# Reordering the head of batch 0 so that norms run ahead of the exps, with 1/rms in PSUM and MLP chunks begun in the score banks

## The chip, the cores and the metric

The kernel runs on one core of one Trainium2 chip. The time is the device time of one execution in microseconds (us), the median of several runs. Each experiment was timed in turns with the kernel before, on the same chip, and is quoted as a ratio to it.

Engines: PE (matmul), PEld (PE's weight loads), DVE (vector), ACT (scalar), POOL (GpSimd), SP (issues DMAs). Each works through its own instructions in order. A *stop* or a *hole* is a stretch in which PE runs nothing.

## The reference, cut to what matters

```python
def _attn_ref(q, k, v, g_q, g_k):          # 8 batches, 12 heads, 448 rows, 64 columns
    def rmsnorm(x, g):
        rms = np.sqrt(np.mean(x * x, axis=-1, keepdims=True) + 1e-06)
        return x / rms * g
    q_n, k_n = (rmsnorm(q, g_q), rmsnorm(k, g_k))
    scores = np.matmul(q_n, k_n.transpose(0, 1, 3, 2)) / np.sqrt(64)
    ...                                    # softmax over the last axis: attn
    return np.matmul(attn, v)

def _moe_ref(x, U, V, w_ch1, w_ch2):       # x: 8 x 448 x 768, w_ch1: 768 x 3072, w_ch2: 3072 x 768
    xt = x.transpose(0, 2, 1)
    h = xt @ U @ V
    u = x + h.transpose(0, 2, 1)
    ch = np.maximum(u @ w_ch1, 0.0) @ w_ch2
    return u + ch
```

Inputs and output are float32.

## The kernel before: the parts that matter here

Two heads make a *pair*, six pairs a batch, two pairs a *tile* of q, k and v loads. A pair needs squares, a sum over the head's columns (`reduce`), 1/rms by Ln and Exp (`rsqrt`), the scaling of q and k (`scale`), a transpose, the scores, the exps, and the product with v (`values`). Batch b+1's attention is woven between the MLP matmuls of batch b. Only batch 0 has nothing to hide behind: pairs 0 to 5 run alone first. That stretch is the *head*. *Mixing* is the U, V part of `_moe_ref`, which makes u; w1 and w2 are `w_ch1` and `w_ch2`. An MLP *chunk* is the six w1 matmuls for 128 of the 3072 hidden columns, with a relu behind them. A *bank* is a PSUM buffer for matmul results; the score banks are those of `ps_s`.

```python
ps_mm = ctx.enter_context(tc.tile_pool(name="ps_mm", bufs=3, space=bass.MemoryType.PSUM))
ps_s  = ctx.enter_context(tc.tile_pool(name="ps_s",  bufs=2, space=bass.MemoryType.PSUM))   # 2 x 2 banks
ps_o  = ctx.enter_context(tc.tile_pool(name="ps_o",  bufs=1, space=bass.MemoryType.PSUM))
...
def scale(p):                               # both inputs in SBUF
    ...
    nc.vector.tensor_tensor(qkns[p]..., qk_of[t][0:SP, a]..., rstds[t][:, a]....to_broadcast([SP, 4, NJ, D]), OP.mult)

def dma_transposes(p):                      # pairs 6 and up
    nc.sync.dma_start_transpose(out=qkTs[p % NQ]..., in_=qkns.pop(p)...)

def gains(p):                               # after a DMA transpose
    qT = blocks(p)[:, :, 0]
    nc.vector.tensor_scalar(qT, qT, gg, None, OP.mult)
...
def pair(p):                                # the head, pairs 0 to 5
    scores(p, (1,)); expo(p, 0)
    if p: values(p - 1, 0)
    if p < 4: scale(p + 1)
    ...
    scores(p, (2,)); expo(p, 1)
    if p < 5: transposes(p + 1)             # on PE
    if p: values(p - 1, 1, ps_mm)
    ...
    if p == 2:                              # the same in pairs 0 and 4
        for a in range(2): reduce(2, a)     # two pairs of norms at once
        rsqrt(2, slice(0, 2))
        ...
    scores(p, (3,)); expo(p, 2)
    ...
    if p < 5: scores(p + 1, (0,))
    expo(p, 3)
```

After the head come `gains(6)`, the six loads of w2, and `mlp(0)` with batch 1's attention woven in.

## Time and profile before

| | before |
|---|---|
| time, median of 3 runs | 640.54 us |
| span of the profiled run | 639.1 us |
| first w1 matmul of batch 0 (end of the head) | 69.6 us |
| first w1 matmul of batch 1 | 148.3 us |
| from there to the end (batches 1 to 7) | 490.8 us |

The page's busy tenths, in 40 slices of 16 us each (PEclk is the granted PE clock in tenths, DMA the busy share of the 16 DMA engines):

```profile
PE   4566598899999999999999999999999999999996
PEclk8555689999999999999999999999999999999999
DMA  8997998442344354373245364265235320050011
```

From the ninth slice on PE is busy and at full clock. The loss is in the slices before: in the first five PE is about half busy, from the second to the fourth at half clock, and DMA is nearly full in the first seven.

The timeline (start, duration, engine, line, operation, in brackets the idle time before it and what ended it) shows one of the head's holes, in pair 2:

```profile
35.56 2.33 DVE L196 TENSOR_REDUCE rstd<-sq 112x16 f32<-112x1024 f32 x2
37.93 0.32 ACT L201 ACTIVATE rstd<-rstd,eps 112x32 f32<-112x32 f32 x1 [6.74 <-DVE rstd L196]
38.41 1.71 ACT L246 ACTIVATE E<-sc 112x896 bf16<-112x896 f32 x2
39.36 0.56 PE L241 MATMUL sc<-qkT 64*128 64x448 bf16 x2 [3.30 <-ACT E L246]
```

Two reductions (2.33 us) stand before Ln and Exp, those stand before the exps, and PE waits 3.3 us for the exps to free the score banks. The same happens in pair 4.

The timeline at the head's end:

```profile
63.22 6.02 SPq L227 DMA_TRANSPOSE qkT<-qkn  x2
69.64 2.13 PE L341 MATMUL ph<-uA,w1b 128*128 128x384 bf16 x6
74.08 0.34 DVE L232 TENSOR_SCALAR qkT<-qkT,gg 128x448 bf16<-128x448 bf16 x1 [5.12 <-DMA qkT<-qkn]
74.48 0.55 PE L241 MATMUL sc<-qkT 64*128 64x448 bf16 x4 [2.71 <-DVE qkT L232]
```

Pair 6 is the first one transposed by DMA. Its transpose was issued at 63.2 us and landed at 74 us, beside the loads of w2.

Batch 1's first w1 matmul, in the view of tile w1b (count, ns min/median/max, first and last start in us):

```profile
L341 PE MATMUL ph<-uB,w1b x138: 377/379/390, 148.3 to 187.6; 128*128 128x512 bf16 x138
```

The groups view: `scale`, with its mean in ns.

```profile
L207 DVE TENSOR_TENSOR qkn<-qk,rstd 112x1024 bf16<-112x1024 f32 x44 | 64.7, 1470 | 2.0 <-ACT rstd L202 2.0
```

### The profile page before, as it was taken

The numbers are of one execution on the slowest core, as the hardware profiler recorded it, in microseconds if no ns is written. First come the engines' busy times: TensorE is split into PE (matmuls) and PEld (weight loads), VectorE is DVE, ScalarE is ACT, GpSimd is POOL, SyncE is SP. The second block draws the span as 40 slices with busy tenths as digits, with TensorE's granted clock in tenths as the row PEclk, the third lists the DMA queues.
The fourth block names the chain that finished last, engine by engine and source line by source line (L and its number), as shares of the span: only waits on it lengthen the run. The fifth ranks groups of instructions, "written<-read, shape, count | busy, mean of one in ns | idle before, by whom it ended". The sixth has DMA issues, their size and how long they took to land.

```text
span 639.1 us, 11042 instructions
## 1 busy us (share of the span) xinstructions
PE 590.5 (92%) x4637; PEld 321.1 (50%) x4658; DVE 333.0 (52%) x656; ACT 235.4 (37%) x361; POOL 143.9 (23%) x110
## 2 busy tenths in 40 slices
PE   4566598899999999999999999999999999999996
PEld 1333245564446555554455655654456555554464
DVE  5455466533765458754665378645465364442211
ACT  3445267404552055505542075406542066202100
POOL 5644336200332003220332022221233000000000
PEclk8555689999999999999999999999999999999999
DMA  8997998442344354373245364265235320050011
GB/s 275 240 257 112 189 210 219 117 100 60 109 128 138 87 125 124 63 198 100 72 125 143 83 153 127 61 168 143 47 107 155 76 56 15 26 100 1 0 50 49
DMA packets 113745, 73.62 MB, mean 115 GB/s; under 512 B 62384, under 2 KB 110112, under 8 KB 113696
## 3 DMA queue, kind: packets, MB, share of 16 engines
q1 hardware_dynamic: 102160, 63.22, 38.7%
q0 software_dynamic: 10944, 9.44, 9.5%
q8 instruction: 36, 0.59, 0.4%
q10 hardware_dynamic: 592, 0.26, 0.1%
q14 instruction: 13, 0.11, 0.1%
HBM read 56.78 MB, written 11.01 MB: 106 GB/s over the span
## 4 chain that ended last, share of the span: by engine, by line
PE 79%; DVE 6%; ACT 1%; issue 1%
PE po L356 35%; PE ph L341 31%; PE o L265 6%; PE sc L241 6%; DVE rstd L196 3%; PE px L315 1%; ACT E L246 1%; DVE x L269 1%; DVE qkT L232 1%; PE pm L294 1%; DVE xs L272 1%; ACT hT L344 0%; DVE osb L360 0%; DVE rec L268 0%; DVE qkn L207 0%
## 5 line engine op out<-in xcount | busy, mean ns | idle before, releaser
L356 PE MATMUL po<-w2b,hT 128*128 128x384 bf16 x1344 | 236.8, 326 | 1.0 <-DVE osb L360 1.0
L246 ACT ACTIVATE E<-sc 112x896 bf16<-112x896 f32 x192 | 168.0, 914 | 75.5 <-PE sc L241 75.4
L356 PEld LDWEIGHTS <-hT 128*128 128x128 bf16 x1344 | 126.7, 98 | 89.4 <-issue 10.2
L341 PEld LDWEIGHTS <-w1b 128*128 128x128 bf16 x1152 | 105.7, 98 | 110.3 <-issue 23.9
L191 POOL TENSOR_TENSOR sq<-qk 112x1024 f32<-112x1024 f32 x42 | 82.5, 1972 | 336.9 <-DMA qk<-in_k_dram 213.3
L344 ACT ACTIVATE hT<-ph 128x384 bf16<-128x384 f32 (+1 forms) x108 | 57.9, 536 | 234.0 <-PE ph L341 233.9
L341 PE MATMUL ph<-uB,w1b 128*128 128x512 bf16 x555 | 131.5, 379 | 1.1
L341 PE MATMUL ph<-uA,w1b 128*128 128x384 bf16 x576 | 108.6, 334 | 0.0
L346 DVE TENSOR_SCALAR hT<-ph 128x512 bf16<-128x512 f32 (+1 forms) x84 | 53.1, 632 | 64.5 <-PE ph L341 63.9
L241 PE MATMUL sc<-qkT 64*128 64x448 bf16 x384 | 60.4, 382 | 25.0 <-ACT E L246 15.9
L265 PEld LDWEIGHTS <-E 112*128 112x128 bf16 x1536 | 64.6, 102 | 19.1 <-issue 3.0
L265 PE MATMUL o<-va,E 112*128 112x65 bf16 x1536 | 69.5, 200 | 1.8 <-DVE xs L272 0.9
L268 DVE RECIPROCAL rec<-o 128x4 f32<-128x4 f32 x96 | 17.4, 181 | 95.9 <-PE o L265 94.9
L360 DVE TENSOR_TENSOR osb<-po,x 128x384 f32<-128x384 f32 x48 | 26.8, 557 | 77.0 <-PE po L356 76.8
L207 DVE TENSOR_TENSOR qkn<-qk,rstd 112x1024 bf16<-112x1024 f32 x44 | 64.7, 1470 | 2.0 <-ACT rstd L202 2.0
L196 DVE TENSOR_REDUCE rstd<-sq 112x16 f32<-112x1024 f32 x48 | 56.1, 1208 | 6.5 <-ACT sq L189 6.2
L241 PEld LDWEIGHTS <-qkT 64*128 64x128 bf16 x384 | 13.1, 95 | 60.5 <-issue 42.0
L269 DVE TENSOR_TENSOR x<-o,rec 128x192 bf16<-128x192 f32 x96 | 34.3, 357 | 3.3
L317 DVE TENSOR_TENSOR x<-px,x 128x384 bf16<-128x384 f32 x48 | 26.1, 554 | 16.1 <-PE px L315 16.0
L181 POOL CAST va<-vt 112x1024 bf16<-112x1024 f32 x23 | 33.8, 1470 | 0.0
L201 ACT ACTIVATE rstd<-rstd,eps 112x32 f32<-112x32 f32 (+1 forms) x25 | 8.0, 321 | 45.0 <-DVE rstd L196 45.0
L232 DVE TENSOR_SCALAR qkT<-qkT,gg 128x448 bf16<-128x448 bf16 x42 | 18.3, 437 | 6.1 <-DMA qkT<-qkn 5.5
(55 smaller groups left out, 160.4 us busy)
## 6 DMA issues: line engine op xcount, KB each, us to landing
vt<-in_v_dram SPq DMA_DIRECT2D x22, 512.0 KB, 5.8
qk<-in_q_dram SPq DMA_DIRECT2D x43, 256.0 KB, 3.9
qk<-in_k_dram SPq DMA_DIRECT2D x42, 256.0 KB, 4.3
w1b<-in_moe_w_ch_dram POOLq DMA_DIRECT2D x6, 768.0 KB, 13.1
w2b<-in_moe_w_ch_dram POOLq DMA_DIRECT2D x6, 768.0 KB, 19.8
out_dram<-osb SPq DMA_DIRECT2D x8, 336.0 KB, 2.9
out_dram<-osb SPq DMA_DIRECT2D x8, 288.0 KB, 2.7
out_dram<-osb SPq DMA_DIRECT2D x8, 240.0 KB, 2.6
```

Source lines behind the costliest of these rows:

```text
L181: nc.gpsimd.tensor_copy(vas[t % NV][:, :, :, 0:D], v_of[t][0:SP].rearrange("p h (j d) -> p h j d", d=D))
L191: nc.gpsimd.tensor_tensor(sqs[t, a], src, src, OP.mult)
L196: nc.vector.tensor_reduce(rstds[t][:, a].rearrange("p h j -> p (h j)"), sqs.pop((t, a)).rearrange("p (g d) -> p g d", d=D), AX, OP.add)
L207: nc.vector.tensor_tensor(qkns[p].rearrange("p j g d -> p g j d"), qk_of[t][0:SP, a].rearrange("p s h (j d) -> p (s h) j d", d=D), rstds[t ...
L241: nc.tensor.matmul(sc[:, hh, 0:S], flat[pp, c:c + P], blocks(p)[pp, :, 0], start=True, stop=True)
L246: nc.scalar.activation(Es[p % NE][:, :, PAD + kc * S:PAD + (kc + 1) * S], scs.pop((p, kc))[0:SP, :, 0:S], AF.Exp, scale=float(D) ** 0.5)
L265: nc.tensor.matmul(o[:, i, :], E[:, hh, c:c + P], va[:, hl, kc, :], start=(kc == 0), stop=(kc == NJ - 1))
L269: nc.vector.tensor_tensor(x3[:, :, d0:d0 + D], o[:, t0:t0 + 3, 0:D], rec[:, t0:t0 + 3].rearrange("p c -> p c ()").to_broadcast([P, 3, D]), ...
L341: nc.tensor.matmul(ph, w1b[:, dc, hc * P:(hc + 1) * P], u[:, dc, :], start=(dc == 0), stop=(dc == KD - 1))
L344: nc.scalar.activation(hT[:, hc, 0:n], ph, AF.Relu)
L346: nc.vector.tensor_relu(hT[:, hc, 0:n], ph)
L356: nc.tensor.matmul(po, hT[:, hc, i * P:(i + 1) * P], w2b[:, hc, hs], start=(hc == 0), stop=(hc == KH - 1))
```

## The change

The intent: in the head one reduction and one rsqrt per pair, two to three pairs ahead, so that no exp stands behind a norm. Pair 6's DMA transpose is issued in pair 4. w1 is loaded from pair 0 on. 1/rms lives in a PSUM bank; for it the values give up their own bank and use the MLP's three. The gain moves from DVE to ACT. The first four MLP chunks begin in the score banks while the head's mixing tail runs. Tile 5 no longer has a buffer of its own, and is loaded after four MLP chunks. The diff, cut to its core:

```diff
-    ps_o = ctx.enter_context(tc.tile_pool(name="ps_o", bufs=1, space=bass.MemoryType.PSUM))
+    ps_r = ctx.enter_context(tc.tile_pool(name="ps_r", bufs=1, space=bass.MemoryType.PSUM))
...
+    rs_bank = ps_r.tile([SP, 6 * 16], FP32, name="rs_bank")
...
-    qk_of = {2: spare_qk(0), 5: spare_qk(16)}
+    qk_of = {2: spare_qk(0)}
...
     def gains(p):
         qT = blocks(p)[:, :, 0]
-        nc.vector.tensor_scalar(qT, qT, gg, None, OP.mult)
+        nc.scalar.activation(qT, qT, AF.Copy, scale=gg)
...
-        if pool is None:
-            o = ps_o.tile([P, 4, D + 1], FP32, tag="o", name="o")
-        else:
-            o = pool.tile([P, 4, D + 1], FP32, tag="mm", name="o")
+        o = ps_mm.tile([P, 4, D + 1], FP32, tag="mm", name="o")
...
     def pair(p):
         scores(p, (1,))
         expo(p, 0)
+        if p == 0:
+            scale(1)
+        elif 1 < p < 5:
+            rsqrt(p + 2)
+        if 0 < p < 5:
+            transposes(p + 1)
...
+        elif p < 5:
+            if p == 1:
+                rsqrt(3)
+            scale(p + 2)
+        if p == 4:
+            dma_transposes(6)
...
         if p == 0:
-            for a in range(2):
-                reduce(1, a)
-            rsqrt(1, slice(0, 2))
...
             load(3)
-            load(5)
+            load_w1(0)
+            cast_v(0)
+            load_w1(1)
+            squares(4)
+            setup_late()
+            load_w1(2)
...
+        if 0 < p < 5:
+            reduce(p + 3)
+            squares(p + 5)
...
+        begin(range(2), range(5))          # five of six matmuls of MLP chunks 0 and 1
         mix_t(0, [slice(5 * P, 6 * P)])
+        begin(range(2, 4), range(5))
         mix_u(5)
+        begin(range(4), (5,))
         gains(6)
+        rsqrt(7)
+        scale(7)
+        dma_transposes(7)
+        reduce(8)
+        squares(10)
+        cast_v(3)
         for half in range(2):
             for i in range(3):
                 load_w2(half, i)
...
             if b == 0:
+                for _ in range(4):
+                    next(fill)
+                load(5)
+                load_v(5)
+                reduce(9)
+                squares(11)
+                rsqrt(8, 2)
...
-                weave(fill, volume(0, 0), items)
-                weave(fill, volume(0, 1) * 0.5, mixing(1))
+                weave(fill, volume(0) * 0.70, items)
+                weave(fill, volume(0) * 0.12, mixing(1))
```

w2 also gets a layout by halves, and batch 0's second layer works through all of half 0 first. Squares of pairs 10 and 11 are computed twice (in the kernel before too).

More of the change, by code (lines that the diff above doesn't have):

```diff
@@ L73 @@
     w1b = consts.tile([P, KD, dh], BF16, name="w1b")
-    w2b = consts.tile([P, KH, dm], BF16, name="w2b")
+    w2b = consts.tile([P, 2, KH, HALF], BF16, name="w2b")
     hT = consts.tile([P, KH, 512], BF16, name="hT")
@@ L91, with rs_of @@
     vL = [consts.tile([P, HG, NJ * D], FP32, name=f"vt{i}") for i in range(2)]
+    rs_bank = ps_r.tile([SP, 6 * 16], FP32, name="rs_bank")
+    def rs_of(p, n=1):
+        c = 16 * (p % 6)
+        return rs_bank[:, c:c + 16 * n]
     spare = hT.rearrange("p k n -> p (k n)").bitcast(FP32)
@@ L96, in spare_qk @@
         return spare[:, k0 * 256:k0 * 256 + 2048].rearrange("p (a s h c) -> p a s h c", a=2, s=2, h=2)
-    qk_of = {2: spare_qk(0), 5: spare_qk(16)}
+    qk_of = {2: spare_qk(0)}
     v_of = {2: spare[:, 8 * 256:12 * 256].rearrange("p (h c) -> p h c", h=HG)}
     for t in range(NT):
-        qk_of.setdefault(t, qkL[(t - (t > 2)) % 2] if t < 5 else qkL[t % 2])
+        qk_of.setdefault(t, qkL[(t - (t > 2)) % 2])
         v_of.setdefault(t, vL[t % 2])
@@ L155, in load_w2 @@
         hs, c = slice(half * HALF, (half + 1) * HALF), slice(8 * i, 8 * (i + 1))
-        nc.gpsimd.dma_start(w2b[:, c, hs], w2r[:, c, hs])
-    sqs, rstds, qkns, scs, x3_of, t4s, us = {}, {}, {}, {}, {}, {}, {}
+        nc.gpsimd.dma_start(w2b[:, half, c], w2r[:, c, hs])
+    sqs, qkns, scs, x3_of, t4s, us, begun = {}, {}, {}, {}, {}, {}, {}
     def heads(x, h, n):
@@ L181, in cast_v, with squares @@
         nc.gpsimd.tensor_copy(vas[t % NV][:, :, :, 0:D], v_of[t][0:SP].rearrange("p h (j d) -> p h j d", d=D))
-    def squares(t, a, eng="pool"):
+    def squares(p, eng="pool", parts=(slice(0, 1024),)):
+        t, a = divmod(p, 2)
         src = qk_of[t][0:SP, a].rearrange("p s h c -> p (s h c)")
-        sqs[t, a] = norm.tile([SP, 2 * 2 * NJ * D], FP32, tag="sq", name="sq")
-        if eng == "act":
-            for s in range(2):
-                c = slice(s * 512, (s + 1) * 512)
-                nc.scalar.activation(sqs[t, a][:, c], src[:, c], AF.Square)
-        else:
-            nc.gpsimd.tensor_tensor(sqs[t, a], src, src, OP.mult)
@@ L193, in reduce @@
-    def reduce(t, a):
-        if t not in rstds:
-            rstds[t] = norm.tile([SP, 2, 4, NJ], FP32, tag="rstd", name="rstd", bufs=3)
-        nc.vector.tensor_reduce(rstds[t][:, a].rearrange("p h j -> p (h j)"),
-                                sqs.pop((t, a)).rearrange("p (g d) -> p g d", d=D), AX, OP.add)
-    def rsqrt(t, pairs):
-        rs = rstds[t][:, pairs].rearrange("p a h j -> p (a h j)")
+        if p not in sqs:
+            sqs[p] = norm.tile([SP, 2 * 2 * NJ * D], FP32, tag="sq", name="sq")
@@ new lines, in squares, with reduce, rsqrt @@
+        for c in parts:
+            if eng == "act":
+                nc.scalar.activation(sqs[p][:, c], src[:, c], AF.Square)
+            else:
+                nc.gpsimd.tensor_tensor(sqs[p][:, c], src[:, c], src[:, c], OP.mult)
+    def reduce(p, parts=(slice(0, 16),)):
+        rs = rs_of(p)
+        sq = sqs[p].rearrange("p (g d) -> p g d", d=D)
+        for c in parts:
+            nc.vector.tensor_reduce(rs[:, c], sq[:, c], AX, OP.add)
+    def rsqrt(p, n=1):
+        rs = rs_of(p, n)
@@ L201, in rsqrt, with scale @@
         nc.scalar.activation(rs, rs, AF.Ln, bias=eps)
         nc.scalar.activation(rs, rs, AF.Exp, scale=-0.5)
-    def scale(p):
+    def scale(p, parts=(slice(0, 4),)):
         t, a = divmod(p, 2)
-        qkns[p] = norm.tile([SP, NJ, 4, D], BF16, tag="qkn", name="qkn", bufs=3)
-        nc.vector.tensor_tensor(
-            qkns[p].rearrange("p j g d -> p g j d"),
-            qk_of[t][0:SP, a].rearrange("p s h (j d) -> p (s h) j d", d=D),
-            rstds[t][:, a].rearrange("p g j -> p g j ()").to_broadcast([SP, 4, NJ, D]),
-            OP.mult)
+        if p not in qkns:
+            qkns[p] = norm.tile([SP, NJ, 4, D], BF16, tag="qkn", name="qkn", bufs=3)
+        for c in parts:
+            n = c.stop - c.start
+            nc.vector.tensor_tensor(
+                qkns[p][:, :, c].rearrange("p j g d -> p g j d"),
+                qk_of[t][0:SP, a].rearrange("p s h (j d) -> p (s h) j d", d=D)[:, c],
+                rs_of(p).rearrange("p (g j) -> p g j ()", j=NJ)[:, c].to_broadcast([SP, n, NJ, D]),
+                OP.mult)
@@ L213, in blocks, with k_side @@
+    def k_side(p):
+        return qkTs[3] if p == 0 else qkTs[p % NQ]
     def blocks(p):
@@ L217, in transposes @@
         qkn = qkns.pop(p)
-        pt = ps_mm.tile([P, NJ, 2, SP], BF16, tag="mm", name="pt")
-        for j in range(NJ):
-            for s in range(2):
-                nc.tensor.transpose(pt[:, j, s], qkn[:, j, 2 * s:2 * s + 2].rearrange("p h d -> p (h d)"),
-                                    ident[:SP, :SP])
-        nc.vector.tensor_scalar(blocks(p)[:, :, 0], pt[:, :, 0], gg, None, OP.mult)
-        nc.vector.tensor_copy(blocks(p)[:, :, 1], pt[:, :, 1])
+        kT = k_side(p)[:, 0:SQK].rearrange("p (j s r) -> p j s r", j=NJ, s=2)[:, :, 1]
+        pt = ps_mm.tile([P, 2, NJ, SP], BF16, tag="mm", name="pt")
+        pts = [pt[:, 0], pt[:, 1]]
+        if p == 0:
+            pts[1] = ps_mm.tile([P, 2, NJ, SP], BF16, tag="mm", name="pt")[:, 0]
+        for s in range(2):
+            for j in range(NJ):
+                nc.tensor.transpose(pts[s][:, j], qkn[:, j, 2 * s:2 * s + 2].rearrange("p h d -> p (h d)"),
+                                    ident[:SP, :SP])
+        nc.vector.tensor_scalar(blocks(p)[:, :, 0], pts[0], gg, None, OP.mult)
+        if p == 0:
+            nc.scalar.copy(kT, pts[1])
+        else:
+            nc.vector.tensor_copy(kT, pts[1])
     def dma_transposes(p):
@@ L231, in gains @@
         qT = blocks(p)[:, :, 0]
-        nc.vector.tensor_scalar(qT, qT, gg, None, OP.mult)
+        nc.scalar.activation(qT, qT, AF.Copy, scale=gg)
     def scores(p, kcs):
-        flat = qkTs[p % NQ]
+        flat, n = k_side(p), SP if p == 0 else P
         for kc in kcs:
@@ L240, in scores @@
                 pp = slice(hh * D, (hh + 1) * D)
-                nc.tensor.matmul(sc[:, hh, 0:S], flat[pp, c:c + P], blocks(p)[pp, :, 0],
+                nc.tensor.matmul(sc[0:n, hh, 0:S], flat[pp, c:c + n], blocks(p)[pp, :, 0],
                                  start=True, stop=True)
@@ L247, in expo, with values @@
                              AF.Exp, scale=float(D) ** 0.5)
-    def values(p, hh, pool=None):
+    def values(p, hh):
         b = p // 6
@@ L257, in values @@
         d0 = (2 * (p % 6) + hh) * D
-        if pool is None:
-            o = ps_o.tile([P, 4, D + 1], FP32, tag="o", name="o")
-        else:
-            o = pool.tile([P, 4, D + 1], FP32, tag="mm", name="o")
+        o = ps_mm.tile([P, 4, D + 1], FP32, tag="mm", name="o")
         for i, off in enumerate(OFFS[par]):
@@ L338, in mlp @@
         for hc in range(KH):
-            ph = ps_mm.tile([P, n], FP32, tag="mm", name="ph")
-            for dc in range(KD):
+            done = 0
+            if (b, hc) in begun:
+                ph, done = begun.pop((b, hc)), KD
+            else:
+                ph = ps_mm.tile([P, n], FP32, tag="mm", name="ph")
+            for dc in range(done, KD):
                 nc.tensor.matmul(ph, w1b[:, dc, hc * P:(hc + 1) * P], u[:, dc, :],
@@ L348, in mlp @@
         xt = x_tiles(b)
-        for i in range(3 + par):
-            off = OFFS[par][i]
-            osb = opool.tile([P, dm], FP32, tag="osb", name="osb")
-            for half in range(2):
-                hs = slice(half * HALF, (half + 1) * HALF)
-                po = ps_mm.tile([P, HALF], FP32, tag="mm", name="po")
-                for hc in range(KH):
-                    nc.tensor.matmul(po, hT[:, hc, i * P:(i + 1) * P], w2b[:, hc, hs],
-                                     start=(hc == 0), stop=(hc == KH - 1))
-                    if hc % 6 == 5 and hc != KH - 1:
-                        yield HALF
-                nc.vector.tensor_add(osb[:, hs], po, xt[i][:, hs])
-                if half == 1:
-                    if off < 0:
-                        store(b - 1, 384, 448, osb, 0)
-                        store(b, 0, 64, osb, 64)
-                    else:
-                        store(b, off, off + P, osb, 0)
-                yield HALF
+        osbs = {}
+        order = [(i, half) for i in range(3 + par) for half in range(2)]
+        if b == 0:
+            order = [(i, half) for half in range(2) for i in range(3)]
+        for i, half in order:
+            off = OFFS[par][i]
+            if i not in osbs:
+                osbs[i] = opool.tile([P, dm], FP32, tag="osb", name="osb")
+            osb = osbs[i]
+            hs = slice(half * HALF, (half + 1) * HALF)
+            po = ps_mm.tile([P, HALF], FP32, tag="mm", name="po")
+            for hc in range(KH):
+                nc.tensor.matmul(po, hT[:, hc, i * P:(i + 1) * P], w2b[:, half, hc],
+                                 start=(hc == 0), stop=(hc == KH - 1))
+                if hc % 6 == 5 and hc != KH - 1:
+                    yield HALF
+            nc.vector.tensor_add(osb[:, hs], po, xt[i][:, hs])
+            if half == 1:
+                if off < 0:
+                    store(b - 1, 384, 448, osb, 0)
+                    store(b, 0, 64, osb, 64)
+                else:
+                    store(b, off, off + P, osb, 0)
+            yield HALF
     def attention(b):
@@ L385, in attention @@
             if t + 2 < NT:
-                if odd:
-                    for a in range(2):
-                        add(0, reduce, t + 2, a)
-                else:
-                    for a in range(2):
-                        add(0, squares, t + 2, a)
+                for a in range(2):
+                    if odd:
+                        add(0, reduce, 2 * t + 4 + a)
+                    else:
+                        add(0, squares, 2 * t + 4 + a)
             add(1, scores, p, (2, 3))
             add(0, expo, p, 2)
-            if odd and t + 2 < NT:
-                add(0, rsqrt, t + 2, slice(0, 2))
             if p % 6:
                 add(1, values, p - 1, 1)
+            if odd and t + 2 < NT:
+                add(0, rsqrt, 2 * t + 4, 2)
             if odd and t + 3 < NT:
@@ L430, in volume, with begin @@
         return first + second if half is None else (first, second)[half]
+    def begin(hcs, dcs):
+        u = u_tile(0)
+        for hc in hcs:
+            if (0, hc) not in begun:
+                pair_of = ps_s.tile([P, 2, 512], FP32, tag="s", name="sc")
+                for k in range(2):
+                    begun[0, hc + k] = pair_of[:, k, 0:384]
+            for dc in dcs:
+                nc.tensor.matmul(begun[0, hc], w1b[:, dc, hc * P:(hc + 1) * P], u[:, dc, :],
+                                 start=(dc == 0), stop=(dc == KD - 1))
@@ L432, in pair @@
     def pair(p):
-        t, odd = divmod(p, 2)
         scores(p, (1,))
         expo(p, 0)
+        if p == 0:
+            scale(1)
[3 more added lines that the diff above has]
+            transposes(p + 1)
+        if p >= 2:
+            mix_t(0, [slice((p - 2) * P, (p - 1) * P)])
         if p:
             values(p - 1, 0)
-        if p < 4:
-            scale(p + 1)
-        if p == 4:
-            scale(5)
-        if p == 5:
-            scale(6)
-            dma_transposes(6)
@@ L448, in pair @@
         scores(p, (2,))
         expo(p, 1)
-        if p < 5:
-            transposes(p + 1)
+        if p == 0:
+            transposes(1)
+            reduce(2)
+        elif p < 5:
[4 more added lines that the diff above has]
+            dma_transposes(6)
         if p:
-            values(p - 1, 1, ps_mm)
+            values(p - 1, 1)
         if p == 0:
-            for a in range(2):
-                reduce(1, a)
-            rsqrt(1, slice(0, 2))
-            for a in range(2):
-                squares(2, a)
-            load(3)
-            load(5)
+            load(3)
+            load_w1(0)
[4 more added lines that the diff above has]
+            load_w1(2)
@@ L462, in pair @@
         if p == 1:
-            load_w1(0)
-            load_w1(1)
-            setup_late()
             cast_v(1)
+            setup_U()
             load_v(3)
-            load_w1(2)
-            setup_U()
+            load_w1(3)
         if p == 2:
-            for a in range(2):
-                reduce(2, a)
-            rsqrt(2, slice(0, 2))
-            for a in range(2):
-                squares(3, a)
+            load_w1(4)
+            cast_v(2)
+            load_w1(5)
             load(4)
@@ L477, in pair @@
             load_v(4)
-            load_w1(3)
-        if p == 3:
-            cast_v(2)
-            load_w1(4)
-            load_w1(5)
-        if p == 4:
-            for a in range(2):
-                reduce(3, a)
-            rsqrt(3, slice(0, 2))
-            for a in range(2):
-                squares(4, a)
-        if p == 5:
-            cast_v(3)
-            scale(7)
-            dma_transposes(7)
-            load_v(5)
+        if 0 < p < 5:
+            reduce(p + 3)
+            squares(p + 5)
@@ L495, in pair @@
         scores(p, (3,))
         expo(p, 2)
-        if p >= 2:
-            mix_t(0, [slice((p - 1) * P, p * P)])
-            if p == 2:
-                mix_t(0, [slice(0, P)])
         if p < 5:
@@ L504, in pair @@
         expo(p, 3)
+        if p == 0:
+            rsqrt(2)
+            scale(2)
+            reduce(3)
+            squares(5)
         if p >= 2:
-            mix_u(p - 1)
-            if p == 2:
-                mix_u(0)
+            mix_u(p - 2)
     with tc.manual_schedule():
+        halves = (slice(0, 512), slice(512, 1024))
+        groups = (slice(0, 8), slice(8, 16))
         load_pair(nc.sync, 0, 0, 0)
@@ L518 @@
         load_v(0)
+        load_mix()
         load(2)
@@ L521 @@
         load_v(2)
-        load_mix()
         setup()
         heat(NWARM)
-        squares(0, 0, "act")
-        reduce(0, 0)
-        rsqrt(0, slice(0, 1))
-        scale(0)
-        squares(0, 1, "act")
-        nc.vector.tensor_mul(gg, gg, gk2)
-        transposes(0)
-        reduce(0, 1)
-        rsqrt(0, slice(1, 2))
-        for a in range(2):
-            squares(1, a)
-        cast_v(0)
+        squares(0, "act", halves)
+        squares(1, "act", halves)
+        reduce(0, groups)
+        rsqrt(0)
+        scale(0, (slice(0, 2), slice(2, 4)))
+        nc.gpsimd.tensor_mul(gg, gg, gk2)
+        transposes(0)
+        reduce(1)
+        rsqrt(1)
+        squares(2)
+        squares(3)
         scores(0, (0,))
@@ L539 @@
             pair(p)
+        mix_t(0, [slice(4 * P, 5 * P)])
         values(5, 0)
-        values(5, 1, ps_mm)
+        mix_u(4)
+        values(5, 1)
+        begin(range(2), range(5))
         mix_t(0, [slice(5 * P, 6 * P)])
+        begin(range(2, 4), range(5))
         mix_u(5)
+        begin(range(4), (5,))
         gains(6)
+        rsqrt(7)
[4 more added lines that the diff above has]
+        cast_v(3)
         for half in range(2):
@@ L550 @@
             if b == 0:
-                for a in range(2):
-                    reduce(4, a)
-                rsqrt(4, slice(0, 2))
-                for a in range(2):
-                    squares(5, a)
+                for _ in range(4):
[5 more added lines that the diff above has]
+                rsqrt(8, 2)
                 extra = [(0, lambda i=i, h=h: mix_x(0, i, h)) for i in range(3) for h in range(2)]
```

## The prediction

> **What bounds the kernel now.** The stretch table shows PE 98 to 100% busy at clock 1.00 from 130 us to 600 us: the rest of the kernel is PE-bound and can gain nothing from this change. The loss is in front. Timeline: the first MLP matmul (w1b) of batch 0 starts at 69.6 us, the first of batch 1 at 148.3 us.
>
> Head (13.6 to 69.6 us): PE is 50 to 84% busy, at clock 0.50 from about 13 to 60 us (values of one head: 1.06 us there, 0.68 us later). Pairs 1 and 3 take about 7.4 us. Pairs 2 and 4 take about 11.7 us, because two reductions (2.33 us), Ln and Exp stand in front of two exps on the in-order engines; the exps resume only at 38.4 and 57.6 us, and PE waits 3.3 us each time. The waits view has ACT waiting 27.3 us on the reductions before 140 us.
>
> Batch 0's MLP (69.6 to 148.3 us): at full clock its PE work is about 63 us (46 us of w1/w2 matmuls, 13 of scores and values, 4 of mixing), so some 15 us are lost. At 71.8 to 74.5 us PE waits for the DMA transpose of pair 6, issued at 63.2 and landed at 74.0 behind the w2 load; then reductions and rsqrt hold back the relus, and the clock stays near 0.5 until about 87 us.
>
> **What the change does.** Each head pair has one reduction and one rsqrt, for pairs two to three ahead; pair 6 is transposed in pair 4, w2 is loaded after it. Per head pair, from trace durations at half clock: PE 6.3 us (scores 2.0, values 2.1, transposes 0.9, mixing 1.3), DVE 5.0 us, ACT 4.4 us. Nothing in the chain then waits for a norm, so I expect 5.5 to 6.7 us a pair. The first exp moves from 13.6 to about 12 us; pair 0 loses its 4 us hole. Head end: 12 + 5 + 5 x 6.2 + 4, about 52 us: 17 us earlier. W1 is loaded from pair 0 on; DMA is saturated until 55 us before (share above 1.1), so this is only just enough.
>
> 1/rms in PSUM: the Trainium skill, "SBUF — State Buffer", Who interferes with whom, says that a DVE instruction with two SBUF inputs contends with a GpSimd one that reads SBUF. The trace agrees: scale takes 1.21 us alone, 2.43 us beside a GpSimd cast or square (mean 1.47). I expect a mean near 1.22 us. This and moving the gain to ACT (0.4 us each) relieve DVE by about 28 us in all, nearly all off the critical path.
>
> Batch 0's MLP: chunks begun in score banks fill the mixing tail (2 us); the attention of batch 1 is spread over 70% of the volume. But load(5) now comes late, beside w2, where such loads took up to 12 us: I expect DVE to wait some us for pair 10's squares. Loss 15 us to about 8.
>
> Cost: the values lose their own bank and share three with the MLP; slack there is tight when two reductions run: +1 to 3 us over batches 1 to 7.
>
> **Sum:** 640.5 - 17 - 8 + 2 = 617 us; 606 to 632. Faster by over 2%: 0.83, within: 0.14, slower: 0.03.
>
> **What would show it:** first w1 matmul at 50 to 56 us; pairs of equal length; batch 1's first w1 matmul near 122 us; no ACT wait on a reduction above 2 us; scale at 1.22 us; PE still 98% busy after 200 us.
>
> **What would make it wrong:** w1 or tile 3 landing late in the saturated DMA; the clock never leaving 0.5 even in the MLP's start; a long DVE wait for load(5); PE stalls from the shared banks in every batch.

## The result, and the profile after

The changed kernel took 632.06 us (median of 4 runs, 629.96 to 632.95) beside 640.2 us for the kernel before; its result is correct. The ratio is 0.9866, 95% interval 0.9836 to 0.9897. Ratios here are the mean time of one kernel's fast runs over that of the other's of the same rounds, so not quite the ratio of the medians quoted. The gain is 8 us (1.3%), not 23, and lies just outside the stated range; "within 2%" had been given 0.14.

```profile
PE   5876788999999999999999999999999999999996
PEclk8668978999999999999999999999999999999999
DMA  8997999564425444464325444454425410050011
```

The first slices are fuller, but slices 4 to 7 (47 to 110 us) still are not at 9.

| from the traces, us | before | after | difference |
|---|---|---|---|
| first w1 matmul of batch 0 | 69.6 | 46.9 | -22.7 |
| from there to batch 1's first w1 matmul | 78.7 | 91.0 | +12.3 |
| from there to the end | 490.8 | 492.8 | +2.0 |
| span | 639.1 | 630.7 | -8.4 |

So the head did what was expected; over half of the gain was given back in the next stage. The border between the two has moved a little: in the changed kernel 20 begun w1 matmuls run before the head's last mixing matmul, which ended at 69.9 us before and at 51.0 us after, 18.8 us earlier. The timeline after:

```profile
39.68 20.52 SPq L249 DMA_TRANSPOSE qkT<-qkn  x2
46.90 1.88 PE L467 MATMUL sc<-uA,w1b 128*128 128x384 bf16 x10
56.66 0.67 ACT L254 ACTIVATE qkT<-qkT,gg 128x448 bf16<-128x448 bf16 x1 [5.14 <-DMA qkT<-qkn]
58.49 0.56 PE L263 MATMUL sc<-qkT 64*128 64x448 bf16 x2 [5.13 <-ACT hT L367]
63.14 5.32 POOL L163 DMA_DIRECT2D w2b<-in_moe_w_ch_dram  x6
72.11 5.59 POOL L199 TENSOR_TENSOR sq<-qk 112x1024 f32<-112x1024 f32 x3 [3.65 <-DMA qk<-in_k_dram]
75.89 1.23 DVE L205 TENSOR_REDUCE rs_bank<-sq 112x16 f32<-112x1024 f32 x1 [4.58 <-POOL sq L199]
79.87 2.10 PE L364 MATMUL ph<-uA,w1b 128*128 128x384 bf16 x6 [5.16 <-DVE xs L291]
103.71 0.36 PE L263 MATMUL sc<-qkT 64*128 64x448 bf16 x2 [2.23 <-ACT qkT L254]
```

and batch 1's first w1 matmul, in the view of tile w1b up to 140 us:

```profile
L364 PE MATMUL ph<-uB,w1b x7: 376/379/390, 137.9 to 140.0; 128*128 128x512 bf16 x7
```

Three stops of PE:

- 53.4 to 58.5 us. Pair 6's transpose, issued at 39.7 us, lands at 56.6 us, 17 us later. For 11.3 us of these SP was still busy with the issuing instruction itself (1.2 us in batches 1 to 7), so the wait is in part one before the DMA engines. ACT stands at its gain; behind that are rsqrt(7) and the relus of the begun chunks. POOL's squares of pair 10 wait in turn for DVE, and w2, behind them on POOL, is issued only at 63.1 us: later than the 60.7 us of before, although the head ended 23 us earlier.
- 74.7 to 79.9 us. Tile 5 was issued at 62.2 us, beside w2, and lands at 72 us. Then POOL does three squares (one of them for nothing), DVE's reduction waits for them, and PE behind DVE.
- 101.5 to 103.7 us: the transpose of pair 10, which landed 20.4 us after its issue.

The chain of waits has these among its longest pieces (start, duration, what). From 40 to 103 us, DMA transposes are most of it (53.9 of 63 us); the chain of the kernel before, which starts at 75.6 us, holds no DMA at all:

```profile
39.68 16.91 DMA qkT<-qkn
64.77 16.63 DMA qkT<-qkn
82.61 20.35 DMA qkT<-qkn
```

Each stop also costs clock. The stretches view (stretch, then its length, busy time of PE, PEld, DVE, ACT and POOL with instruction counts, and last the granted clock, DMA share and GB/s):

```profile
70.00:75.00 5.00, 4.70 (x53) 2.58 (x50) 0.77 (x3) 2.46 (x5) 2.89 (x2) 1.00 1.47 199
75.00:80.00 5.00, 0.13 (x1) 0.13 (x2) 3.38 (x6) 0.43 (x2) 3.68 (x3) 0.78 1.28 132
80.00:85.00 5.00, 4.19 (x14) 1.42 (x13) 1.53 (x2) 3.04 (x5) 0.00 (x0) 0.50 1.28 192
85.00:90.00 5.00, 5.00 (x36) 2.61 (x34) 1.33 (x4) 2.12 (x4) 0.00 (x0) 0.69 1.23 244
```

After 5 us without work PE is at 0.50 and takes until about 88 us to recover. The Trainium skill, "TensorE: Matmul & The Clock Gate", What's actually happening, describes this: half clock after an idle window of about 3.4 us, full clock again after a busy one. This trace agrees, and shows why the recovery took 8 us. The granted clock changed only at steps of 3.41 us, and full clock came after the first step that PE filled; 76% of the one before it had not been enough:

```profile
77.82:81.23 3.41, 1.36 (x5) 0.69 (x6) 3.30 (x6) 0.43 (x2) 0.86 (x1) 0.50 1.09 163
81.23:84.65 3.42, 2.61 (x10) 0.71 (x9) 0.30 (x1) 3.04 (x5) 0.00 (x0) 0.50 1.27 191
84.65:88.06 3.41, 3.41 (x18) 1.79 (x17) 0.00 (x0) 1.48 (x3) 0.00 (x0) 0.50 1.24 236
88.06:91.47 3.41, 3.41 (x46) 2.06 (x44) 1.97 (x7) 2.11 (x4) 1.44 (x1) 1.00 1.22 250
```

A PE that reads "busy" in such a stretch does half the work: the twelve w1 matmuls from 83.8 us on took 4.02 us, twelve at full clock (217.4 us) 2.06 us.

The groups view for `scale`:

```profile
L218 DVE TENSOR_TENSOR qkn<-qk,rs_bank 112x1024 bf16<-112x1024 f32 x45 | 54.6, 1213 | 10.4 <-ACT rs_bank L210 10.1
```

1213 ns, as predicted; DVE's busy time fell from 333.0 to 305.7 us. Neither shortened batches 1 to 7 (492.8 us against 490.8).

### The profile page after: what moved, and what is told of

It is laid out like the page before. It is cut to its first block, busy times and chain, and to the rows that moved or that the text cites. A ratio compares the mean times of both kernels' runs of the same rounds, so it can differ in the third digit from the quotient of the medians.

```text
span 630.7 us, 11153 instructions
## 1 busy us (share of the span) xinstructions
PE 592.5 (94%) x4637; PEld 321.7 (51%) x4658; DVE 305.7 (48%) x614; ACT 257.6 (41%) x410; POOL 130.0 (21%) x111
## 4 chain that ended last, share of the span: by engine, by line
PE 75%; DMA 13%; DVE 7%; ACT 2%; issue 1%; POOL 0%; SPq 0%; DVEq 0%; ACTq 0%; POOLq 0%
PE po L384 33%; PE ph L364 29%; DMA qkT<-qkn 9%; PE sc L263 6%; PE o L284 5%; DVE rs_bank L205 4%; DMA qk<-in_k_dram 4%; PE px L334 1%; ACT E L268 1%; PE pm L313 1%; DVE hT L369 1%; ACT hT L367 1%; DMA uB<-x 1%; DVE x L288 1%; ACT qkT L254 0%
## 5 line engine op out<-in xcount | busy, mean ns | idle before, releaser
L384 PE MATMUL po<-w2b,hT 128*128 128x384 bf16 x1344 | 239.7, 328 | 1.3 <-DVE osb L388 1.3
L268 ACT ACTIVATE E<-sc 112x896 bf16<-112x896 f32 x192 | 170.4, 916 | 76.2 <-PE sc L263 75.9
L199 POOL TENSOR_TENSOR sq<-qk 112x1024 f32<-112x1024 f32 x46 | 86.7, 1892 | 348.4 <-DMA qk<-in_k_dram 291.5
L364 PE MATMUL ph<-uA,w1b 128*128 128x384 bf16 x552 | 105.1, 337 | 5.6 <-DVE xs L291 5.2
L205 DVE TENSOR_REDUCE rs_bank<-sq 112x16 f32<-112x1024 f32 (+1 forms) x49 | 58.9, 1201 | 17.5 <-POOL sq L199 9.4
L218 DVE TENSOR_TENSOR qkn<-qk,rs_bank 112x1024 bf16<-112x1024 f32 (+1 forms) x47 | 55.9, 1191 | 11.0 <-ACT rs_bank L210 10.7
L263 PEld LDWEIGHTS <-qkT 64*128 64x128 bf16 (+1 forms) x384 | 14.1, 97 | 49.7 <-issue 37.9
L336 DVE TENSOR_TENSOR x<-px,x 128x384 bf16<-128x384 f32 x48 | 25.9, 554 | 18.9 <-PE px L334 18.8
L254 ACT ACTIVATE qkT<-qkT,gg 128x448 bf16<-128x448 bf16 x42 | 27.8, 662 | 9.5 <-DMA qkT<-qkn 9.5
L188 POOL CAST va<-vt 112x1024 bf16<-112x1024 f32 x23 | 23.8, 1039 | 1.7 <-DMA vt<-in_v_dram 1.7
L291 DVE TENSOR_TENSOR xs<-o,rec 64x64 bf16<-64x64 f32 x96 | 20.8, 217 | 0.7
```

The costliest lines, as they stand in the source:

```text
L199: nc.gpsimd.tensor_tensor(sqs[p][:, c], src[:, c], src[:, c], OP.mult)
L205: nc.vector.tensor_reduce(rs[:, c], sq[:, c], AX, OP.add)
L218: nc.vector.tensor_tensor(qkns[p][:, :, c].rearrange("p j g d -> p g j d"), qk_of[t][0:SP, a].rearrange("p s h (j d) -> p (s h) j d", d=D) ...
L254: nc.scalar.activation(qT, qT, AF.Copy, scale=gg)
L263: nc.tensor.matmul(sc[0:n, hh, 0:S], flat[pp, c:c + n], blocks(p)[pp, :, 0], start=True, stop=True)
L268: nc.scalar.activation(Es[p % NE][:, :, PAD + kc * S:PAD + (kc + 1) * S], scs.pop((p, kc))[0:SP, :, 0:S], AF.Exp, scale=float(D) ** 0.5)
```

## The experiments

Theory **T**: the DMA transposes of pairs 6 and up land late, because they share the DMA engines with w1 and w2, and three engines stand in order behind them. Theory **L**: the late load of tile 5 is a second, separate wait. Rivals: **A**, the gain on ACT holds back the relus; **V**, the bytes of w1 and w2 alone set the time; **P**/**S**, the shared PSUM banks. All runs are of three rounds; the kernel before took 642.2 to 642.6 us (medians) in them, so ratios are to be compared, not times. The changed kernel was timed in a session of its own; with both intervals a difference of a run's ratio to its 0.9866 is uncertain by about 0.004, or 2.6 us, so smaller differences are not told from noise.

| run | ratio to before | first w1 matmul, batch 0 | batch 1 | batches 1 to 7 |
|---|---|---|---|---|
| changed kernel | 0.9866 | 46.9 | 137.9 | 492.8 |
| e1_pe_t6 | 0.9747 | 47.3 | 131.0 | 492.9 |
| e2_gain_dve | 0.9818 | 46.2 | 136.5 | 492.3 |
| e3_w2_early | 0.9836 | 46.0 | 136.6 | 492.8 |
| e4_half_weights | 0.9679 | 45.7 | 128.5 | 492.8 |
| e5b_load5_early | 0.9769 | 45.9 | 131.3 | 492.8 |
| e6b_t6_load5 | 0.9742 | 47.1 | 127.4 | 492.9 |
| e7b_all_pe_t | 0.9633 | 47.9 | 124.9 | 492.7 |
| e8b_own_bank | 0.9775 | 46.7 | 136.8 | 490.0 |
| e9_w1_later | 0.9799 | 40.1 | 133.4 | 492.8 |
| e10_best | 0.9488 | 45.6 | 117.8 | 489.9 |
| e11_pe_own | 0.9549 | 49.2 | 126.2 | 489.9 |
| e12_rs_sbuf | 0.9789 | 49.7 | 134.7 | 490.8 |

The last three columns are us in the profiled run of each; the fourth is the span less the third.

### Pair 6 transposed on PE

```diff
-        if 0 < p < 5:
+        if 0 < p < 6:
             transposes(p + 1)
-        if p == 4:
-            dma_transposes(6)
...
-        gains(6)
```

> Pair 6 is transposed on PE like pairs 1 to 5; its DMA transpose and the gain on ACT behind it are gone. Theory T (the transposes by DMA land 15 to 20 us late behind the weight loads, and PE, ACT and DVE stand in order behind them): the hole of PE at 53.4 to 58.5 us goes, w2 is issued about 5 us earlier, 624 to 628 us against 632 of the changed kernel; the later transposes still land late. Rival V (the bytes of w1 and w2 alone set when batch 0's MLP ends, whoever waits for what): 630 to 633 us unless w2 moves. Rival P (the values and begun chunks that share PSUM banks cost it): 631 to 633 us.

Measured: 626.28 us, ratio 0.9747 (0.9711 to 0.9783). The stop at 53 us shrank to 1.35 us, w2 was issued at 57.6 us in place of 63.1, and batch 1 began 6.9 us earlier. The stop for tile 5 stayed (3.9 us, at 70.6 to 74.5 us). As T said; P would have seen nothing. Where the stop of 5.13 us had been:

```profile
57.88 0.36 PE L263 MATMUL sc<-qkT 64*128 64x448 bf16 x2 [1.35 <-ACT E L268]
```

### The gain back on DVE

```diff
-        nc.scalar.activation(qT, qT, AF.Copy, scale=gg)
+        nc.vector.tensor_scalar(qT, qT, gg, None, OP.mult)
```

> The multiplication by the gain goes back from ACT to DVE, everything else as in the changed kernel. Rival A (the gain on ACT holds the relus of the begun chunks back while its transpose is late): PE goes on with MLP chunks, 626 to 629 us. Theory T: the scores of pair 6 stand next on PE and need the same transpose, so the hole at 53 to 58 us stays, 631 to 634 us.

Measured: 630.91 us, ratio 0.9818 (0.9793 to 0.9843), between the two expectations. The timeline of this run:

```profile
58.19 0.34 DVE L254 TENSOR_SCALAR qkT<-qkT,gg 128x448 bf16<-128x448 bf16 x1 [9.63 <-DMA qkT<-qkn]
58.58 0.93 PE L263 MATMUL sc<-qkT 64*128 64x448 bf16 x4 [5.98 <-DVE qkT L254]
```

The stop is there and even longer, with DVE as the one that waits. So which engine holds the gain does not matter to it: A falls as the cause. The gain on ACT may cost some 3 us elsewhere (difference of the ratios, 0.5%, with intervals that overlap).

### w2 issued earlier

```diff
+        for half in range(2):
+            for i in range(3):
+                load_w2(half, i)
         gains(6)
         ...
         cast_v(3)
-        for half in range(2):
-            for i in range(3):
-                load_w2(half, i)
```

> w2 is issued ahead of the squares of pair 10 and the cast of v, so at about 54 us and not at 63 us, which fills the 8 us in which the DMA engines are idle. Rival V: 623 to 626 us, for w2 ends 8 us earlier. Theory T: 628 to 632 us, for the transposes of pairs 7 to 9 still land 15 to 20 us after issue.

Measured: 631.45 us, ratio 0.9836 (0.981 to 0.9862). w2 was issued at 53.0 us, 10 us earlier, and its last part landed at 89.8 us in place of 107.8, yet batch 1 began only 1.3 us earlier: V falls. The early w2 made other DMAs late: stops of 5.3 us at 52 us, 2.4 us at 66 us and 4.7 us at 79 us.

### Half of the weights

```diff
-                nc.tensor.matmul(ph, w1b[:, dc, hc * P:(hc + 1) * P], u[:, dc, :],
+                nc.tensor.matmul(ph, w1b[:, dc, hc % 12 * P:(hc % 12 + 1) * P], u[:, dc, :],
...
-                nc.tensor.matmul(po, hT[:, hc, i * P:(i + 1) * P], w2b[:, half, hc],
+                nc.tensor.matmul(po, hT[:, hc, i * P:(i + 1) * P], w2b[:, 0, hc],
```

and `load_w1(3)` to `load_w1(5)` and the second half of w2 are not loaded. The result is wrong (relative error 0.66).

> Wrong result on purpose: half of w1 and half of w2 are loaded and used twice, the same matmuls. Theories T and V (both DMA): the DMA transpose of pair 6 lands within 5 us, no PE hole over 2 us from 46 to 130 us, batch 1's first w1 matmul near 118 us, 610 to 617 us. Rivals A and P (ACT order, banks, no DMA): 628 us or more.

Measured: 621.63 us, ratio 0.9679 (0.9653 to 0.9705). Pair 6's transpose, issued at 39.3 us, had landed when ACT came to it at 50.1 us; the DMA engines were idle from 45 to 50 us. The stop at 53 us was gone. But a stop of 6.45 us remained, which was not expected: tile 5, issued at 55.7 us, still took until 66.4 us beside half of w2, and its three squares (5.6 us) did the rest. So the total lies between the two ranges, and batch 1 began at 128.5 us, not near 118. Both stops begin with a late DMA, and halving the bytes cures only one. That the weights make pair 6's transpose late is shown; by which path is not: SP's q and k loads issued before it landed earlier too (41.6 us, not 51.6), so whether the transpose waits for DMA engines or behind the loads of its own queue stays open.

### Tile 5 loaded early

```diff
-    qk_of = {2: spare_qk(0)}
+    qk_of = {2: spare_qk(0), 5: spare_qk(16)}
...
+        if p == 5:
+            load(5)
...
-        squares(10)
...
-                load(5)
-                squares(11)
```

with the buffers of later tiles as in the kernel before.

> From the changed kernel: q and k of tile 5 (pairs 10 and 11) get a buffer of their own again and are loaded in pair 5 of the head, not after four chunks of the MLP; the two squares that were computed twice are computed once. Theory L (the late load beside w2, then three squares on GpSimd in front of the reduction, stop DVE and PE at 74.7 to 79.9 us and cool the clock until about 87 us): that hole goes, the hole at 53 to 58 us stays; ratio to the kernel before 0.971 to 0.977 (622 to 626 us). Rival (only the transposes by DMA count): 0.984 to 0.988, unchanged.

Measured: 626.79 us, ratio 0.9769 (0.9741 to 0.9796). The stop at 75 us was gone; the one before it grew to 7.9 us (52.2 to 60.1 us). L holds: a second cause, worth about 6 us (0.9866 - 0.9769, times 640). But the edit did more than load early: without `squares(10)` ahead of it, w2 was issued at 54.2 us in place of 63.1, and POOL had two squares to do, not three. The 6 us belong to all of it. The stop that grew:

```profile
60.09 0.56 PE L263 MATMUL sc<-qkT 64*128 64x448 bf16 x2 [7.86 <-ACT hT L367]
```

### Both remedies

> Both remedies, pair 6 on PE and the early load of tile 5. If the two waits are separate causes, their gains add: ratio 0.957 to 0.966 (614 to 619 us). If one only uncovers the other: not below 0.970.

Measured: 624.6 us, ratio 0.9742 (0.9686 to 0.9798, one of the four runs at 630). The gains did not add. The timeline shows why:

```profile
72.37 15.59 SPq L249 DMA_TRANSPOSE qkT<-qkn  x2
92.80 0.67 ACT L254 ACTIVATE qkT<-qkT,gg 128x448 bf16<-128x448 bf16 x1 [5.48 <-DMA qkT<-qkn]
93.52 0.56 PE L263 MATMUL sc<-qkT 64*128 64x448 bf16 x2 [5.17 <-ACT qkT L254]
```

With the first two stops away PE came sooner to pair 10, and stopped 5.2 us for its transpose, which was again 20.4 us late. In the changed kernel it had cost 2.2 us; the rest had been hidden by the waits that were removed.

### All of batch 1's pairs transposed on PE

The same, and `transposes(p)` in place of `dma_transposes(p)` and `gains(p)` for pairs 7 to 11.

> As the last one, and pairs 7 to 11 are transposed on PE too, so that no DMA transpose stands beside w2. If the transposes of these pairs still cost waits (hole near 103 us, 11 to 20 us from issue to landing): a further 3 to 6 us, ratio 0.950 to 0.959. If they are hidden: the same as the last within 2 us, or 2 us slower, for about 3 us of PE work were added.

Measured: 618.78 us, ratio 0.9633 (0.959 to 0.9675): 6 to 7 us below the last (by the medians, by the ratios), although PE has more to do. The forecast of a further 3 to 6 us held; its absolute range was missed because the last step's was. Batch 0's stage took 77.1 us (47.9 to 124.9 us), 13.9 us less than in the changed kernel: more than the 12.3 us by which that stage had grown. From 46 us on, one PE stop over 1.1 us is left:

```profile
59.69 0.36 PE L263 MATMUL sc<-qkT 64*128 64x448 bf16 x2 [1.56 <-ACT E L268]
```

### The values' own bank, and 1/rms in SBUF

```diff
-    rs_bank = ps_r.tile([SP, 6 * 16], FP32, name="rs_bank")
+    rs_bank = consts.tile([SP, 6 * 16], FP32, name="rs_bank")
...
-        o = ps_mm.tile([P, 4, D + 1], FP32, tag="mm", name="o")
+        o = (ps_r if p >= 6 else ps_mm).tile([P, 4, D + 1], FP32, tag="o" if p >= 6 else "mm", name="o")
```

> From the changed kernel: 1/rms goes back from PSUM to SBUF, and from batch 1 on the values have one PSUM bank of their own again, as before the change. Theory S (sharing three banks with the MLP costs the 2 us that batches 1 to 7 grew by): those batches take 490.8 us again and not 492.8; scale is 1.45 us again where GpSimd works beside it. Whole kernel within 0.5% of the changed one, ratio 0.982 to 0.989. Rival (the 2 us have another source): batches 1 to 7 stay at 492.8.

Measured: 627.41 us, ratio 0.9775 (0.9743 to 0.9807), a larger gain than expected; batches 1 to 7 took 490.0 us. `scale` was 1533 ns. That looked like S. But two things had been undone, so the last run undid one, 1/rms in SBUF with the values still in the shared banks:

> From the changed kernel: 1/rms goes back to SBUF, but the values go on sharing the three banks with the MLP; the freed bank lies idle. This splits the run that had both. Theory S (sharing costs batches 1 to 7 about 2.5 us): they take 492 to 493.5 us, as in the changed kernel, and scale is slower again beside GpSimd (mean 1.5 us, not 1.21). Rival (it was 1/rms in PSUM that cost them): 490 us. Whole kernel 0.984 to 0.989.

Measured: 627.79 us, ratio 0.9789 (0.9736 to 0.9842), `scale` 1526 ns, and batches 1 to 7 at 490.8 us. So S falls for the larger part: of 2.8 us, 2.0 came from 1/rms in PSUM and 0.8 from the shared banks (undone in this order; the other order was not run). There is one profile of each, but the nine kernels with both took 492.3 to 492.9, and the difference repeats from batch to batch: batches 1, 3 and 5, each from its first w1 matmul to the next batch's, take 77.9 us in the changed kernel, 77.5 here and 77.3 with the own bank, with a spread of at most 0.03 us within a kernel. In the timeline of the changed kernel, and then of this one, the two reductions of a tile:

```profile
312.43 2.54 DVE L205 TENSOR_REDUCE rs_bank<-sq 112x16 f32<-112x1024 f32 x2
```

```profile
308.22 2.33 DVE L204 TENSOR_REDUCE rs_bank<-sq 112x16 f32<-112x1024 f32 x2
```

Two reductions into the PSUM bank take 0.2 us longer than two into SBUF, but a single one is hardly slower. The source view of the two lines, changed kernel first:

```profile
L205 DVE TENSOR_REDUCE rs_bank<-sq x49: 695/1227/1229, 5.5 to 511.6; 112x16 f32<-112x1024 f32 x47, 112x8 f32<-112x512 f32 x2
L205 DVEq EVENT_SEMAPHORE  x24: 21/21/21, 6.2 to 511.5; - x24
L204 DVE TENSOR_REDUCE rs_bank<-sq x49: 676/1209/1220, 5.4 to 506.2; 112x16 f32<-112x1024 f32 x47, 112x8 f32<-112x512 f32 x2
```

With 1/rms in PSUM a semaphore wait (EVENT_SEMAPHORE) stands on DVE between the two: the second starts 0.10 us after the end of the first, in SBUF 0.08 us before it. ACT has such waits too in front of Ln (28 against 1). That these waits are the way in which PE loses the 2 us is argued, not shown. Both runs' ratios lie under the stated ranges. The rest of this run's gain lies in batch 0, where its load timing differed: its stops at 56 and 75 us were 2.9 and 2.7 us; why is left open.

### w1 later

```diff
             load(3)
-            load_w1(0)
             cast_v(0)
-            load_w1(1)
             squares(4)
             setup_late()
-            load_w1(2)
...
             squares(5)
+            load_w1(0)
+            load_w1(1)
...
             load_v(3)
+            load_w1(2)
             load_w1(3)
```

> From the changed kernel: the first w1 loads are issued at about 22 us, behind the squares of pair 5, not from 12 us on, so that the q and k of tile 3 go through the saturated DMA first. Theory D (the 3.4 us hole of PE at 33.7 to 37.1 us comes from tile 3 landing late behind w1): the hole goes, the head ends 2 to 4 us earlier; but pair 6's transpose then stands behind the later w1 and lands no earlier than 56 us, so most of it is given back: 629 to 632 us, ratio 0.982 to 0.987. Rival (the hole has another source): hole unchanged.

Measured: 629.39 us, ratio 0.9799 (0.9764 to 0.9834). This is the clearest of the runs for the transposes. The head's last hole (3.4 us at 37 us, tile 3 late behind w1) went, and the first w1 matmul came at 40.1 us, 6.8 us earlier than in the changed kernel. Then:

```profile
34.62 23.68 SPq L249 DMA_TRANSPOSE qkT<-qkn  x2
40.09 1.79 PE L467 MATMUL sc<-uA,w1b 128*128 128x384 bf16 x10
54.76 0.67 ACT L254 ACTIVATE qkT<-qkT,gg 128x448 bf16<-128x448 bf16 x1 [10.13 <-DMA qkT<-qkn]
56.59 0.56 PE L263 MATMUL sc<-qkT 64*128 64x448 bf16 x2 [10.13 <-ACT hT L367]
```

The transpose was issued 5 us earlier and landed 2 us earlier; PE's stop doubled to 10.1 us. A head that is 7 us shorter moves PE's return by 2 us: where this transpose lands follows the DMA traffic more than the time of its issue. Theory D holds, with two sizes off: the head gained more than 2 to 4 us, and the transpose landed before 56 us. Batch 1 began 4.5 us earlier, so less was given back than expected and the ratio lies under its range.

### All remedies

Pairs 6 to 11 on PE, tile 5 early, 1/rms in SBUF, the values' own bank; once without and once with w1 later and `reduce(8)` ahead of `scale(7)`:

> The same without w1 later and without the moved reduction. Theory S: 2 to 3 us under the all-PE-transposes kernel, ratio 0.957 to 0.961; batches 1 to 7 take 490 us where sharing banks took 492.8.

> All remedies together: pairs 6 to 11 transposed on PE, tile 5 loaded early, 1/rms in SBUF and a bank of their own for the values, w1 later, and the reduction of pair 8 ahead of the scale of pair 7. If the gains add: 2 to 3 us from the bank, 2 to 3 us from w1, 1 us from the reduction below the all-PE-transposes kernel (ratio 0.963), so 0.952 to 0.958 (611 to 615 us).

Measured: 613.41 us, ratio 0.9549 (0.9507 to 0.9591), without, and batches 1 to 7 in 489.9 us; 609.18 us (608.51 to 609.47), ratio 0.9488 (0.9455 to 0.952), with. Both are a little better than expected. Both results are correct; the latter beats the kernel before by 33 us and the changed one by about 24 (0.9866 - 0.9488, times 640). Its batch 1 begins at 117.8 us. Its page:

```profile
PE   5688999999999999999999999999999999999996
PEclk8789999999999999999999999999999999999999
DMA  8999998643353643641454443634444311140011
```

PE is at 9 from the fifth slice on, though the DMA line is as full as ever: nearly the same bytes (72.3 MB, before 73.6), and in the chain of waits up to batch 1 no DMA transpose of q and k is left.

## Why the prediction was wrong

- *Head end about 52 us, 17 us earlier.* Right in mechanism, and about right in size: the last mixing matmul ended at 51.0 us, 18.8 us earlier, and the first w1 matmul, now begun ahead of it, came at 46.9 us, 22.7 us earlier; first exp at 10.9 us, not 12. PE waits for exps behind norms were gone. One hole stayed (3.4 us), of the kind that was named: tile 3 late behind w1; the w1-later run showed it. The good fit is partly luck: the sum had no such hole, but it also took half clock for the whole head, and PE had full clock from 26.6 to 36.9 us.
- *"Batch 0's MLP: loss 15 us to about 8."* **This is the step that failed.** The stage grew from 78.7 to 91.0 us; against the estimated 63 us of PE work the loss is 28 us, not 8. The term left out is the latency of DMA transposes while weights are loading. With pairs 6 to 11 transposed on PE and tile 5 loaded early the stage took 77.1 us. The prediction had the number in hand (10.8 us for pair 6 before) and took it that issuing in pair 4 cures it. It does not: the transpose then stands beside w1, and took 17 us; those of later pairs stood beside w2 and took up to 20 us. "DMA is saturated" was read as a question of whether w1 arrives in time; it did. What suffered were the transposes and the loads of tile 5 beside the weights.
- *w2 "is loaded after it".* True in program order, but w2 was issued 2.4 us later than before, for POOL stood behind squares, those behind DVE, that behind ACT, and ACT behind the transpose.
- *load(5) late: "some us".* Right in mechanism: a stop of 5.2 us, and half clock until about 88 us; the early load, with the superfluous squares removed and w2 issued 9 us earlier for it, was worth 6 us.
- *Scale at 1.22 us, DVE relieved by 28 us, off the critical path.* Right: 1.21 us, 27.3 us (333.0 - 305.7), no gain. The reason is as the Trainium skill, "SBUF — State Buffer", Who interferes with whom, says: with 1/rms back in SBUF (the last run that undid it alone) `scale` took 1.22 us where no POOL instruction overlapped it and 1.99 us on average where one did; with 1/rms in PSUM 1.21 us either way.
- *+1 to 3 us in batches 1 to 7.* Right in size (2.0) by luck, wrong in cause: undoing 1/rms in PSUM gave 2.0 us and undoing the shared banks 0.8, so the rest of the change must have gained some 0.8 us there.

The forecast for batch 1's first w1 matmul, 122 us, was approached by the versions without DMA transposes beside the weight loads (124.9 and 126.2 us) and beaten only by the one that also loads w1 later (117.8 us).

## What to carry to other kernels

When a stage is made shorter, list every small DMA that the next stage's first instruction needs, and ask what bulk load it shares the engines with: its latency under load sets when it lands, and an earlier issue need not help. If an idle engine can do the same thing (here PE, 0.57 us for a pair's eight transposes), take it off DMA while the weights come in. Expect gains from removing waits not to add: look for the wait that each one was hiding, and count the clock that every long PE stop costs afterwards.

## What the Trainium skill lacked or had wrong

- "DMA: Bandwidth & Descriptors", Issuing engines are not separate DMA queues, says that DMAs from all issuing engines share 16 DMA engines and interleave. The runs agree, but the page gives no size for what a small transfer then suffers: the same SBUF transpose landed after 2.9 us in batches 1 to 7 (median) and after 15 to 20 us for five of the six pairs from 6 to 11 in the changed kernel, beside w1 or w2 (2.9 us for pair 7, issued between the two).
- The same page, DMA Transpose (X-bar), lists TensorE among the alternative paths, as useful when the data is already on the chip, and says nothing of how a DMA transpose fares beside bulk loads. Here TensorE was the better one under load: moving pairs 7 to 11 to PE took about 6 us off the kernel (624.6 to 618.8) with more PE work.
- "VectorE: DVE Perf Modes", The TRN2 errata, has a cycle table for DVE that reads SBUF or PSUM and writes SBUF, but no column for a result written to PSUM: here a reduction took 1.227 us into PSUM and 1.209 us into SBUF (medians).
- "TensorE: Matmul & The Clock Gate", What's actually happening, gives at least one busy window of about 3.4 us for the return to full clock and at least one idle window for its loss, but not how busy or idle a window has to be. Counted in steps of 3.41 us between changes of the granted clock, up to the last return to full clock near the end of batch 0, in the 14 profiles: of 65 half-clock steps with PE under 80% busy none was followed by full clock, of 44 with PE busy throughout 43 were; of 35 full-clock steps with PE under 40% busy all were followed by half clock, of 102 with PE over 70% busy none was. (PE's ends are modelled in the profile.)
